# A transformer block kernel re-ordered: projections and V products between logit rounds, DMA transposes, an order computed at build

## Chip, cores, metric

The kernel runs on one core of one Trainium2 chip. The metric is the device time of one execution in microseconds (us). Every timed run quoted below was classed as fast, that is, none was more than 1.5% above the fastest of its kernel. The core's clock is the granted clock of TensorE, as a share of full speed. Engines are named as in the profile: PE is the matrix engine (PEld its weight loads, which overlap), DVE the vector engine, ACT the scalar engine, POOL GpSimd, SP the queue that issues DMAs.

## The reference, cut to what matters

```python
# x: [2048, 1024]; 32 heads of 32, 4 segments of 512 tokens, attention inside a segment
q, k, v = ln(x) @ wq, ln(x) @ wk, ln(x) @ wv
for s in range(4):
    logits = qs @ ks.T * scale + causal_mask           # 512 x 512 per head
    a_dot  = softmax(logits) @ vs
    a_mem  = (phi(qs) @ M) / (phi(qs) @ z + 1e-6)      # phi(t) = t + 1 if t > 0 else exp(t)
    o      = g * a_mem + (1 - g) * a_dot               # g = sigmoid(beta), per head
    M, z   = M + phi(ks).T @ vs, z + phi(ks).sum(tokens)
h  = x + o @ wo
z  = gelu(ln(h) @ w_in)                                # 3584 wide, halves z1 and z2
h2 = h + (z1 * (w_sp @ ln(z2) + b_sp)) @ w_out         # w_sp: 2048 x 2048 over tokens
```

Everything is bf16 with f32 accumulation. Both kernels use the same large matmuls. Counted in matmuls of 128x128 by 512 columns there are 768 for q, k and v, 256 for the output projection, 896 for w_in, 896 for w_sp and 448 for w_out: 3264 in all.

## The kernel before

Each engine's stream is written by hand. Attention works on a head group of four heads at a time (eight groups per segment). A group has four logit rounds (key blocks j = 0..3). Each round puts four heads' logits into four PSUM banks, adds the causal mask by a matmul of the identity with a triangle, and has ACT exponentiate all four banks. The next round needs the same banks, so it waits for that exponential.

```python
def L(j):                                     # one logit round of a head group
    for i in range(4):                        # four heads, side by side in the array
        P("pe", matmul(bank_f32(LB[i])[:, 0:nj], kT[32*i:32*(i+1), c, j*128:(j+1)*128],
                       qT[32*i:32*(i+1), c, 128*j:512], start=True, stop=False))
    for i in range(4):                        # the mask, added by PE
        tp = P("pe", matmul(bank_f32(LB[i])[:, 0:128], IDENT, NEGTRI, start=False, stop=True))
    ta = P("act", activation(ESALL[:, :, OFFJ[j]:...], PS[:, 0:4, 0:nj], Exp, scale=SCALE), waits=[tp])
# ...
L(0); run_extra(1)                            # extra: projections etc. of the NEXT segment
L(1); PV_emit(0); run_extra(1)                # PV_emit(cq): V product and combine of a quarter
L(2); PV_emit(1); run_extra(1)
L(3); PV_emit(2); PV_emit(3)                  # + update of M
run_extra(len(xu))

for s in range(NSEG):
    # extra units exist only where a next segment exists: segment 3 has none
    for cq_ in range(NQ):
        quad(s, cq_, per_quad[cq_])
    seg_end(s)      # 4 x (transpose 128 rows of o on PE, copy on DVE, output projection, add, store)
# w_in: two DMAs of 3.5 MB, the first released when segment 2 is done
```

All transposes (x, phi(k), o, h, w_sp) are PE transposes followed by a copy out of PSUM.

The softmax here doesn't subtract the row's maximum and nothing guards it: scores larger than these inputs give would overflow.

## Time and profile before

Median 1139.18 us of 3 runs (1135.2 to 1139.63).

From the page of the kernel before: the engine table (busy time, share of the span, instructions) and the chain of work that ended last, by engine.

```profile
PE 947.2 (83%) x6735; PEld 483.9 (42%) x6848; DVE 527.8 (46%) x1448; ACT 304.3 (27%) x383; POOL 35.2 (3%) x68
...
PE 68%; DVE 15%; ACT 6%; DMA 4%; issue 4%; POOL 1%; SPq 0%; DVEq 0%; ACTq 0%; POOLq 0%
```

The view of stretches cuts the span into the stages: start, attention up to the end of segment 2, segment 3 and its output projection, the gate layer (w_in), and the rest (w_sp and w_out). The columns are the stretch, its length, busy time of each engine with instruction counts, the granted clock, the DMA share and GB/s.

```profile
core 0: us, PE busy (x) PEld busy (x) DVE busy (x) ACT busy (x) POOL busy (x), PEclk, DMA share, GB/s
0.00:25.70 25.70, 4.16 (x33) 3.11 (x34) 13.29 (x36) 1.51 (x2) 8.12 (x21) 1.00 0.88 317
25.70:450.00 424.30, 343.99 (x3299) 182.54 (x3353) 226.71 (x750) 193.69 (x228) 8.40 (x14) 0.89 0.08 27
450.00:596.00 146.00, 87.08 (x791) 49.02 (x800) 74.11 (x268) 40.88 (x33) 1.66 (x3) 0.66 0.20 71
596.00:825.00 229.00, 209.16 (x1107) 106.89 (x1128) 99.66 (x227) 68.24 (x120) 17.05 (x30) 0.95 0.13 42
825.00:1140.20 315.20, 302.82 (x1508) 142.33 (x1536) 114.03 (x168) 0.00 (x0) 0.00 (x0) 0.99 0.16 47
```

The reader should see two things. The last two stages are nearly PE-bound at nearly full clock. The first 596 us are not: PE idles a quarter of them, and in segment 3 it also runs at two thirds of its clock.

The waits of PE name what it stood still for (total us, times, longest). Summed over the whole list, not only the five lines shown, PE waits 53.8 us for exponentials (28.0 of the 50.3 below in segment 3) and 111.4 us for DVE.

```profile
engine line waited for: us in total, times, longest us
PE ps L506 <- ACT eall L520: 50.3, 47, 2.0
PE ps L386 <- DVE oT L652: 21.6, 16, 3.1
PE ps L339 <- DVE xn_89 L352: 15.2, 4, 8.4
PE ps L339 <- DVE hn_109 L746: 13.2, 5, 7.2
PE ps L876 <- DMA wspch_115<-in_B_w_sp_dram: 10.5, 2, 6.0
```

L506 is the logits, L520 the exponential, L652 the copy of transposed o, L339 a transpose behind a layer norm. A piece of the timeline of PE in segment 3 shows what a round looks like there; in square brackets stands the idle time before the group and what ended it.

```profile
504.60 0.61 PE L506 MATMUL ps<-qT_70,kT_72 32*128 32x512 bf16 x4
505.14 0.61 PE L513 MATMUL ps<-negtri,ident 128*128 128x128 bf16 x4
507.72 0.51 PE L506 MATMUL ps<-qT_70,kT_72 32*128 32x384 bf16 x4 [1.97 <-ACT eall L520]
508.16 0.60 PE L513 MATMUL ps<-negtri,ident 128*128 128x128 bf16 x4
508.98 0.32 PE L551 MATMUL ps<-v_76,eall 128*128 128x33 bf16 x4 [0.22 <-issue]
510.31 0.40 PE L506 MATMUL ps<-qT_70,kT_72 32*128 32x256 bf16 x4 [1.00 <-ACT eall L520]
```

Waits of about 2 and 1 us stand between pieces of 1 us of work, and the work itself is slow: the clock is at 0.50.

**A ledger.** The span is split in three, from the view of stretches at 5 us steps: *idle* is the length less PE busy; *cold* is PE busy times (1 minus the granted clock), summed; *work* is the remaining PE busy. For the kernel before: idle 192.7, cold 69.4, work 877.9 us. The split is rough where records are missing (the page of e1 below shows 5261 of 5358 matmuls) and where the clock is low (e12 below shows an error of 26 us), so small differences in it prove nothing.

### The profile page before, as it was taken

How to read it: one execution, taken by the hardware profiler on the slowest of the kernel's cores; microseconds unless marked ns; L12 is line 12 of the kernel's file. 1: busy time of each engine (PE TensorE's matmuls, PEld its weight loads, DVE VectorE, ACT ScalarE, POOL GpSimd, SP SyncE). 2: the span in 40 equal slices, each digit the busy share in tenths (PEclk: the TensorE clock that was granted, in tenths of full speed). 3: DMA queues.
4: the chain of work that ended last, by engine and by line, in shares of the span. 5: the costliest groups of instructions: out<-in, count | busy, mean ns of one | idle time of the engine just before them, and what ended most of it. 6: DMA issues, size and time to landing. Idle time of an engine off the chain costs nothing.

```text
span 1140.2 us, 16027 instructions
## 1 busy us (share of the span) xinstructions
PE 947.2 (83%) x6735; PEld 483.9 (42%) x6848; DVE 527.8 (46%) x1448; ACT 304.3 (27%) x383; POOL 35.2 (3%) x68
## 2 busy tenths in 40 slices
PE   2978886688775898566749999999599999999998
PEld 1444443444333443233324545444344444444443
DVE  4066333886447853366454553632344253343332
ACT  0356651366313652144202333333100000000000
POOL 2000000000000000000000000100000000000000
PEclk9988989798985999765678999999799999999999
DMA  8010002000020004400021000000610310301102
GB/s 324 26 29 1 1 1 83 29 1 1 1 93 20 1 1 163 169 1 1 19 92 29 19 19 19 20 1 1 238 53 1 92 61 13 112 29 37 42 1 65
DMA packets 23305, 54.53 MB, mean 48 GB/s; under 512 B 2369, under 2 KB 6977, under 8 KB 23233
## 3 DMA queue, kind: packets, MB, share of 16 engines
q1 hardware_dynamic: 19152, 34.10, 9.6%
q0 software_dynamic: 4080, 19.40, 4.5%
q8 instruction: 54, 0.88, 0.3%
q14 instruction: 19, 0.15, 0.0%
HBM read 45.10 MB, written 8.39 MB: 47 GB/s over the span
## 4 chain that ended last, share of the span: by engine, by line
PE 68%; DVE 15%; ACT 6%; DMA 4%; issue 4%; POOL 1%; SPq 0%; DVEq 0%; ACTq 0%; POOLq 0%
PE ps L386 33%; PE ps L902 17%; PE ps L929 8%; ACT eall L520 4%; PE ps L513 3%; DVE stats L323 3%; PE ps L506 2%; DMA wqkv<-in_A_wv_dram 2%; PE ps L551 2%; PE ps L876 1%; DVE ta L579 1%; DVE tm L581 1%; POOL sm_58 L328 1%; PE ps L556 1%; PE ps L339 1%
## 5 line engine op out<-in xcount | busy, mean ns | idle before, releaser
L520 ACT ACTIVATE eall<-ps 128x2048 bf16<-128x2048 f32 (+3 forms) x128 | 158.6, 1239 | 173.0 <-PE ps L513 172.4
L386 PE MATMUL ps<-xnT,wqkv 128*128 128x512 bf16 x489 | 118.6, 388 | 11.3 <-DVE msum L635 4.6
L929 PE MATMUL ps<-w_out,yT 128*128 128x512 bf16 x437 | 96.8, 379 | 6.9 <-DVE yT L908 6.4
L902 PE MATMUL ps<-wspT_113,z_106 128*128 128x512 bf16 x439 | 99.1, 386 | 1.7 <-DVE wspT_113 L879 1.3
L902 PE MATMUL ps<-wspT_114,z_106 128*128 128x512 bf16 x440 | 96.6, 379 | 0.4
L905 DVE TENSOR_TENSOR tmpg<-ps,brow_120 128x512 f32<-128x512 f32 x56 | 38.7, 692 | 118.4 <-PE ps L902 103.6
L386 PE MATMUL ps<-wo,oT 128*128 128x512 bf16 x248 | 63.9, 412 | 21.8 <-DVE oT L652 21.6
L323 DVE BATCH_NORM_STATS2 stats<-z2g 128x6 f32<-128x448 bf16 x64 | 35.3, 614 | 90.9 <-ACT z2g L818 90.9
L386 PEld LDWEIGHTS ps<-xnT,wqkv 128*128 128x128 bf16 x512 | 47.3, 99 | 62.4 <-DVE msum L635 5.8
L929 PEld LDWEIGHTS ps<-w_out,yT 128*128 128x128 bf16 x448 | 43.5, 98 | 60.2 <-DVE yT L908 8.2
L902 PEld LDWEIGHTS ps<-wspT_113,z_106 128*128 128x128 bf16 x448 | 44.0, 99 | 53.9 <-issue 3.6
L902 PEld LDWEIGHTS ps<-wspT_114,z_106 128*128 128x128 bf16 x448 | 43.7, 98 | 51.9
L818 ACT ACTIVATE z2g<-ps 128x512 bf16<-128x512 f32 x64 | 34.8, 544 | 111.4 <-PE ps L386 111.4
L386 PE MATMUL ps<-wqkv,xnT 128*128 128x512 bf16 x248 | 59.0, 391 | 4.5 <-DVE msum L635 3.6
L513 PE MATMUL ps<-negtri,ident 128*128 128x128 bf16 x512 | 61.6, 256 | 0.0
L506 PE MATMUL ps<-qT_70,kT_72 32*128 32x512 bf16 (+3 forms) x256 | 25.0, 380 | 33.6 <-ACT eall L520 33.6
L386 PE MATMUL ps<-w_in_hi,hnT_103 128*128 128x512 bf16 (+1 forms) x251 | 51.6, 364 | 1.4 <-DVE hnT_103 L760 1.2
L818 ACT ACTIVATE z1T<-ps 128x512 bf16<-128x512 f32 x56 | 33.4, 597 | 70.7 <-PE ps L386 70.7
L386 PE MATMUL ps<-hnT_104,w_in_lo 128*128 128x512 bf16 x217 | 49.4, 379 | 0.4
L386 PE MATMUL ps<-w_in_hi,hnT_104 128*128 128x512 bf16 (+1 forms) x253 | 49.6, 352 | 0.2
L386 PE MATMUL ps<-hnT_103,w_in_lo 128*128 128x512 bf16 x218 | 49.3, 379 | 0.3
L386 PEld LDWEIGHTS ps<-wo,oT 128*128 128x128 bf16 x256 | 25.6, 104 | 55.2 <-issue 13.4
(138 smaller groups left out, 1073.5 us busy)
## 6 DMA issues: line engine op xcount, KB each, us to landing
wspch_115<-in_B_w_sp_dram SPq DMA_DIRECT2D x8, 512.0 KB, 4.1
wspch_122<-in_B_w_sp_dram SPq DMA_DIRECT2D x8, 512.0 KB, 4.2
hr_0_121<-out_dram SPq DMA_DIRECT2D x16, 256.0 KB, 2.8
w_in_lo<-in_B_w_in_dram POOLq DMA_DIRECT2D x1, 3584.0 KB, 12.2
w_in_hi<-in_B_w_in_dram POOLq DMA_DIRECT2D x1, 3584.0 KB, 22.8
w_out<-in_B_w_out_dram POOLq DMA_DIRECT2D x1, 3584.0 KB, 17.8
xch_87<-in_A_x_dram SPq DMA_DIRECT2D x8, 256.0 KB, 2.8
xch_88<-in_A_x_dram SPq DMA_DIRECT2D x8, 256.0 KB, 3.0
```

Source lines behind the costliest of these rows:

```text
L323: t = P("dve", (lambda e, ci=ci: e.bn_stats(STATS[:, ci, :], eng_in_ap[:, ci * csz:(ci + 1) * csz])), waits=((list(first_wait) + [chain["l ...
L328: tp = P("pool", lambda e: e.tensor_tensor(SM4[:, 1:2], SM4[:, 0:1], MHALF[:], ALU.pow), waits=[t], sig=g_pool)
L339: tok = P("pe", (lambda e, i=i: e.transpose(bb[:, i * 128:(i + 1) * 128], src_tile[:, col0 + i * 128: col0 + (i + 1) * 128], IDENT[:])), w ...
L386: tok = P("pe", (lambda e, i=i: e.matmul(dst, lhs_of_i(i), rhs_of_i(i), start=(i == 0), stop=(i == 7))), waits=(waits if i == 0 else []), ...
L506: P("pe", (lambda e, i=i, dst=dst: e.matmul(dst, kT[32 * i:32 * (i + 1), c, j * 128:(j + 1) * 128], qT[32 * i:32 * (i + 1), c, 128 * j:512 ...
L513: tp = P("pe", (lambda e, dstd=dstd: e.matmul(dstd, IDENT[:], NEGTRI[:], start=False, stop=True)), sig=(g_pe_act if i == 3 else None))
L520: ta = P("act", (lambda e: e.activation(dst4, src4, ACTF.Exp, scale=float(SCALE))), waits=wa, sig=g_act_pe)
L551: fn = (lambda e, i=i, j=j, h=h: e.matmul(dstb[:, i * 128:i * 128 + 33], ESALL[:, i, OFFJ[j] + (cq - j) * 128: OFFJ[j] + (cq - j + 1) * 12 ...
L818: t4 = P("act", (lambda e, dst=dst, o=blk["out"]: e.activation(o, dst, ACTF.Gelu_apprx_tanh)), waits=[tp] + wz, sig=g_act_dve)
L902: tok = P("pe", (lambda e, sc=sc, fc=fc, dst=dst: e.matmul(dst, Z2[:, sc, fc * 128:(fc + 1) * 128], wb[:, sc, :], start=(sc == 0), stop=(s ...
L905: t1 = P("dve", lambda e, dst=dst: e.tensor_tensor(TMPG[:], dst, BROW[0][:], ALU.add), waits=[tok, _w16(tb), tmpg_res.free], sig=g_dve_pe)
L929: tok = P("pe", (lambda e, fc=fc, half=half, tcl=tcl, dst=dst: e.matmul(dst, YT[:, fc, tcl * 128:(tcl + 1) * 128], WOUT[:, fc, half * 512: ...
```

## The change

The intent: keep PE fed throughout. The attention loop runs one head group ahead with q and k and one behind with the V product, so that each of its three logit rounds (the two shortest are merged) has independent PE work behind it. V of the next segment and the output projection of the last one are spread one group per round. The mask moves from PE to POOL, transposes go by DMA, w_in is loaded in eight blocks under segment 3, and the memory product is 132 columns wide in place of 512. PE's order is the program's; the orders of ACT, DVE, POOL and SP are computed at build by a list schedule with a cost for each operation, and the waits follow from tracked memory ranges.

```diff
+    def schedule(self):                      # at build; PE in program order, others by readiness
+        lag_same, lag_x = 30.0, 55.0
+        ... heap per engine, priority = program position ...
+            if o.dma:
+                free[e] = start + 60.0       # assumed time to issue a DMA, ns
+    def pts1(o, i, s, op):                   # assumed: 0.98 us for 1024 elements on POOL
+        G.op(POOL, ..., (150 + n_of(o)) / 1.2, name="pts1")
...
-            tp = P("pe", matmul(dstd, IDENT, NEGTRI, start=False, stop=True))
+        act(E[n % 2][...], PS[:, 0:4, 0:w], ACTF.Exp, scale=float(SCALE))
+        for j in js:                         # mask after the exponential, on POOL
+            G.op(POOL, affine_select(d, d, [[0, 4], [1, 128]], ALU.is_ge, 0.0, ...), ..., 550)
...
+    def phi(n):
+        act(ex[:, lo:hi, :], q[:, lo:hi, :], ACTF.Exp)
+        pts1(ex[:, lo:hi, :], ex[:, lo:hi, :], 1.0, ALU.min)       # POOL
+        stt(PKT[n % 2][:], q[:, 1, :], 1.0, ex[:, 1, :], ALU.add, ALU.max)
+        dma(PK[n % 3][:], PKT[n % 2][:], transpose=True)
...
+    for n in range(32):                      # n = 8 * segment + head group
+        if s >= 1 and c == 2:
+            wo_q += [(s - 1, g) for g in range(8)]                 # then one per round
+        logits(n, 0)
+        Pq(n + 1)                            # query product of the next group
+        X(n - 1)                             # V product of the last group, quarters 0 to 2
+        logits(n, 1)
+        Pk(n + 1)
+        MZU(n - 1)                           # quarter 3, memory product, update, combine
+        logits(n, 2)
+        phi(n + 1)
+        for a in vs:  v_group(*a)            # V of the next segment
+        for a in wos: wo_group(*a)           # output projection of the last segment
+        if n < 4: x_norm(4 + n)
+        if s <= 1 and c >= 4: x_norm(4 * (s + 2) + c - 4)
+        if s == 3: ... win_load(k) ...       # w_in in 8 blocks
```

(The whole kernel was rewritten in this style.)

## The prediction

> **What bounds it now.** The engine table has PE busy 947 of 1140 us (83%); the chain of waits runs over PE for 68% of the span, DVE 15%, ACT 6%, DMA 4%. Stretches: start 26 us (PE busy 4), attention to about 596 us (PE busy 431 of 570, clock 0.66 from 450 to 596), first gate layer about 596 to 809, token mixing and output layer 825 to 1140 at clock 0.96 to 1.00. Full-speed matmuls of 512 columns come every 0.216 us (49 in 10.74 us, one record in 50 missing). The last 500 us are nearly PE-bound.
>
> **Losses named by the wait list (PE).** For the exponentials 50 us, output-projection transposes through DVE 22, layer-norm chains 15+13+10+8, w_in and first weights: PE does 1.5 of 10 us from 455 to 465 while DMA moves 370 GB/s. Segment 3 has nothing between its logit rounds: 10.2 us per four heads, PE half cold (clock 0.50 from 505 to 565).
>
> **Removed from PE.** 512 mask matmuls of 128 columns (about 28 us of streaming), some 700 of 736 transposes of 128 columns (39 us), memory product 512 to 132 columns (96 times 0.16, 15 us). w_in arrives under segment 3; x, V, output projection and the last group's PV sit between logit rounds.
>
> **PE work after, at full clock (estimates from trace durations).** 3264 matmuls of 512 columns (or equivalent) x 0.2157 = 704; logits 32 x 0.95 = 30; 1280 PV matmuls x 0.045 (16 in 0.72 us) = 58; memory products and updates 12; 32 transposes 2. Sum 806.
>
> **Added around it.** Start about 9 us before the first V product plus about 4 of cold clock; last addition and store 4; waits for the last y of each block 5; gaps 5. Attention per four heads in the middle segments: PE about 10 us; ACT 0.6x3 + 1.04 + 1.88 + 1.45x2 = 7.6 us; DVE about 7.5 us; POOL about 5 us (not measured in this trace). PE should stay the bound, but only four banks rotate there, and the reciprocal-POOL-DVE chain of combine holds them: I allow 25 us of stalls. Total about 858 us.
>
> **The clock.** The Trainium skill (TensorE: Matmul & The Clock Gate, Part 1) says that an idle window drops the clock to half and that sustained work restores it. The trace agrees: 0.50 where PE sits idle over 2 us per round, 1.00 from 905 on. With dense rounds I expect 0.97 or more on average.
>
> **DMA transposes.** The skill (DMA: Bandwidth & Descriptors, latency table) gives 261 GB/s for transposes with a non-contiguous middle dimension. By estimate 0.5 us for 128 KB, 8 us per 2 MB block of w_sp plus a couple of us latency; all have 10 us or more of slack.
>
> **What would show it.** PE over 93% busy and clock over 0.96; waits for exponentials under 10 us; attention with last output projection ending near 370 us; gate layer about 193 us; mixing and output about 295 us; DMA share low.
>
> **What would make it wrong.** DMA transposes much slower, or occupying the SP queue so that loads behind them are late; POOL masking slower than about 1 us per call, or DVE and POOL blocking each other, so that combine sets the period (12 us instead of 10 would add 60 us); PE clock falling in segments 0 and 3, where rounds are thinner.
>
> Faster by over 2%: 0.98; within 2%: 0.01; slower: 0.01. Time 860 us, 8 in 10 between 830 and 920.

## The result

Median 849.34 us of 4 runs (848.38 to 850.28) against 1139.41 of 4 (1135.2 to 1140.14). The ratio is 0.7454, 95% interval 0.7431 to 0.7476. A ratio is the mean time of one kernel's fast runs over that of the other's of the same rounds, so it is not quite the ratio of the medians quoted.

The page of the changed kernel, engine table and chain by engine:

```profile
PE 800.9 (94%) x5358; PEld 384.5 (45%) x5358; DVE 368.2 (43%) x813; ACT 299.0 (35%) x343; POOL 223.2 (26%) x353
...
PE 77%; DVE 8%; POOL 7%; DMA 4%; issue 2%; ACT 2%; SPq 1%
```

Its stretches: start; attention up to the first gate product; the gate layer, which also holds the last head group's V product and the last output projection; and the rest.

```profile
core 0: us, PE busy (x) PEld busy (x) DVE busy (x) ACT busy (x) POOL busy (x), PEclk, DMA share, GB/s
0.00:15.80 15.80, 2.09 (x17) 1.76 (x18) 9.83 (x21) 1.51 (x2) 3.58 (x13) 1.00 0.89 273
15.80:345.00 329.20, 299.43 (x2914) 148.83 (x2913) 200.47 (x511) 229.25 (x221) 202.78 (x296) 0.97 0.43 106
345.00:554.00 209.00, 209.00 (x1071) 101.60 (x1070) 73.20 (x138) 67.64 (x119) 16.86 (x44) 1.00 0.25 57
554.00:847.80 293.80, 290.33 (x1359) 132.28 (x1357) 84.71 (x145) 0.60 (x1) 0.00 (x0) 1.00 0.18 46
```

From 345 us on, PE never stops until the last store. Attention shrank from some 570 us to about 330, without the last V product and output projection (some 16 us, now inside the gate layer), and its clock is 0.97.

What PE still waits for:

```profile
engine line waited for: us in total, times, longest us
PE ps L437 <- DVE xin L454: 13.7, 2, 7.9
PE ps L428 <- DMA oT<-oq: 12.2, 2, 6.8
PE ps L433 <- ACT e L440: 7.1, 6, 2.2
PE ps L428 <- DVE ta L460: 5.7, 7, 1.5
PE ps L428 <- POOL e L591: 3.5, 5, 1.4
```

The wait for the exponentials (L433 on L440) fell from 50.3 to 7.1 us. The first line is the start (the layer norm of the first x chunks). The second is new and is explained below.

The ledger of both kernels, worked out as above:

| us | before | after | difference |
|---|---|---|---|
| idle | 192.7 | 47.1 | -146 |
| cold | 69.4 | 7.0 | -62 |
| work at full clock | 877.9 | 793.9 | -84 |
| sum | 1140 | 848 | -292 |

So by this split roughly three tenths of the gain are matmuls that PE no longer does, half is idle time, and a fifth is clock that PE no longer loses. Of the idle time, waits for exponentials fell from 53.8 to 7.1 us and waits for DVE from 111.4 to 19.4. The experiments ask which part of the change removes which of these.

Two more readings of the changed kernel matter. The first is what POOL's operations cost. The groups of POOL: busy us and mean ns of one, then idle before and its releaser.

```profile
L591 POOL TENSOR_SCALAR_AFFINE_SELECT e<-e 128x512 bf16<-128x512 bf16 x128 | 93.3, 743 | 17.2 <-ACT e L440 17.2
...
L474 POOL TENSOR_SCALAR ex<-ex 128x1024 bf16<-128x1024 bf16 x16 | 44.4, 2773 | 1.5 <-ACT ex L440 0.5
```

The minimum of phi takes 2.77 us where the schedule reckons (150 + 1024) / 1.2 = 978 ns. A mask takes 0.743 us where it reckons 0.55.

The second is the longest wait for oT, in the timelines of SP and of PE:

```profile
205.06 1.19 SPq L481 DMA_TRANSPOSE pk<-pkt  x1
206.30 1.26 SPq L481 DMA_TRANSPOSE oT<-oq  x1
```

```profile
208.86 3.36 PE L428 MATMUL ps<-wo,oT 128*128 128x512 bf16 x8 [6.81 <-DMA oT<-oq]
```

This wait should not exist. The eight output-projection groups of segment 0 are popped one per round from group 2 of segment 1, so the eighth runs in round n = 17. The program text of that round puts MZU(16) ahead of it, and MZU(16) writes the o of segment 2's first heads into the same buffer (OT[s % 2]). The dependence tracker therefore makes the eighth group wait for that new o, and the trace shows it waiting: oT is issued at 206.30, PE resumes at 208.86. The kernel pays 6.8 us (and 5.4 us at the next boundary) to read a buffer that has just been overwritten; the eight matmuls after the wait then take 3.36 us, where the same eight took 1.89 a round earlier. A second slip of this kind is in the last lines of the loop: x_norm for segment s + 2 is emitted from c = 4 on and overwrites parts of the xnT buffer that the query and key products of head groups 6 and 7 of segment s, still to come, read. The trace shows this order too: the transposes of segment 2's first two chunks are issued at 75.23 and 83.17 us, the query products of head groups 6 and 7 of segment 0 follow at 78.53 and 86.25, and the first of them waited 0.25 us for that transpose. By the program, both make parts of the attention output wrong. The comparison with the reference passes all the same; no run measured the size of the error, and these are not races: every access is ordered, only in the wrong order.

### The profile page after: what moved, and what is told of

Same layout as the page of the kernel before. It is cut to its first block, busy times and chain, and to the rows that moved or that the text cites. A ratio compares the mean times of both kernels' runs of the same rounds, so it can differ in the third digit from the quotient of the medians.

```text
span 847.8 us, 12679 instructions
## 1 busy us (share of the span) xinstructions
PE 800.9 (94%) x5358; PEld 384.5 (45%) x5358; DVE 368.2 (43%) x813; ACT 299.0 (35%) x343; POOL 223.2 (26%) x353
## 2 busy tenths in 40 slices
DMA packets 128313, 64.80 MB, mean 76 GB/s; under 512 B 95488, under 2 KB 120064, under 8 KB 128256
## 4 chain that ended last, share of the span: by engine, by line
PE 77%; DVE 8%; POOL 7%; DMA 4%; issue 2%; ACT 2%; SPq 1%
PE ps L428 75%; POOL ex L474 5%; DMA xin<-in_A_x_dram 2%; PE ps L433 2%; DVE stats L512 1%; DVE pq L463 1%; DVE oq L460 1%; DVE pkt L463 1%; POOL e L591 1%; ACT e L440 1%; DVE hx L460 1%; ACT ex L440 1%; POOL rs L470 1%; DVE ta L460 1%; DMA oT<-oq 1%
## 5 line engine op out<-in xcount | busy, mean ns | idle before, releaser
L428 PE MATMUL ps<-wspT,z 128*128 128x512 bf16 x896 | 194.0, 379 | 0.0
L440 ACT ACTIVATE e<-ps 128x1536 bf16<-128x1536 f32 (+1 forms) x96 | 152.3, 1587 | 56.6 <-PE ps L433 56.5
L428 PEld LDWEIGHTS ps<-wspT,z 128*128 128x128 bf16 x896 | 87.7, 98 | 105.7
L440 ACT ACTIVATE z<-ps 128x512 bf16<-128x512 f32 x120 | 68.2, 569 | 144.7 <-PE ps L428 144.7
L591 POOL TENSOR_SCALAR_AFFINE_SELECT e<-e 128x512 bf16<-128x512 bf16 x128 | 93.3, 743 | 17.2 <-ACT e L440 17.2
L428 PE MATMUL ps<-win,hnT 128*128 128x512 bf16 (+1 forms) x512 | 97.8, 352 | 0.0
L428 PE MATMUL ps<-wout,y 128*128 128x512 bf16 (+2 forms) x462 | 97.4, 373 | 0.0
L428 PE MATMUL ps<-hnT,win 128*128 128x512 bf16 x448 | 97.3, 379 | 0.0
L428 PE MATMUL ps<-wo,oT 128*128 128x512 bf16 x256 | 63.6, 400 | 12.2 <-DMA oT<-oq 12.2
L474 POOL TENSOR_SCALAR ex<-ex 128x512 bf16<-128x512 bf16 (+1 forms) x32 | 68.5, 2142 | 18.8 <-ACT ex L440 17.1
L428 PE MATMUL ps<-xnT,wq 128*128 128x512 bf16 x256 | 62.7, 389 | 0.3 <-DMA xnT<-xin 0.3
L428 PEld LDWEIGHTS ps<-v,e 128*128 128x128 bf16 x1280 | 41.1, 96 | 13.9 <-POOL e L591 4.0
```

The source lines that it names most:

```text
L428: G.op(PE, lambda e: e.matmul(o, lhsT, rhs, start=start, stop=stop), [lhsT, rhs], [o], max(n, 60) / 2.4, lag=166, name="mm")
L440: G.op(ACT, lambda e: e.activation(o, i, func, scale=scale), [i], [o], ((172 if inps(i) else 224) + n_of(i)) / 1.2, prio=prio, name=str(func))
L474: G.op(POOL, lambda e: e.tensor_single_scalar(o, i, s, op), [i], [o], (150 + n_of(o)) / 1.2, name="pts1")
L591: G.op(POOL, lambda e, d=d: e.affine_select(d, d, [[0, 4], [1, 128]], ALU.is_ge, 0.0, base=0, channel_multiplier=-1), [d], [d], 550, name= ...
```

## The experiments

All are edits of the changed kernel, timed over 3 rounds (4 runs each), all correct by the comparison. Differences are of medians, from 849.34. The runs were on several chips; the kernel before, timed beside each, had medians from 1137.26 to 1140.12, so a difference of some 3 us says nothing.

| run | edit | median us | range | ratio to before | difference |
|---|---|---|---|---|---|
| e1 | eighth output projection one round earlier | 839.01 | 837.65 to 842.79 | 0.7372 | -10.3 |
| e2 | minimum of phi on DVE | 832.37 | 831.2 to 834.38 | 0.7311 | -17.0 |
| e3 | e1, and x norms after the last reader | 838.8 | 837.42 to 840.47 | 0.7366 | -10.5 |
| e4 | e2 and e3, x loaded first | 825.28 | 824.8 to 827.91 | 0.7253 | -24.1 |
| e5 | V and output projection clustered | 890.4 | 889.34 to 891.92 | 0.782 | +41.1 |
| e6 | V product in its own round | 864.07 | 862.12 to 865.46 | 0.7582 | +14.7 |
| e7 | mask back on PE | 872.0 | 870.51 to 872.77 | 0.7656 | +22.7 |
| e8 | x, h, w_sp transposed on PE | 896.72 | 895.05 to 901.75 | 0.7882 | +47.4 |
| e9 | w_in after attention | 856.3 | 854.5 to 859.13 | 0.7529 | +7.0 |
| e10 | e5 to e9 together | 967.39 | 966.72 to 968.12 | 0.8503 | +118.1 |
| e11 | schedule with measured costs | 836.11 | 834.83 to 839.47 | 0.7346 | -13.2 |
| e12 | e10, and projections in one burst per segment | 1101.2 | 1100.32 to 1101.84 | 0.9668 | +251.9 |

Two theories ran through them. One: PE is the bound and the change works by filling PE's waits and shedding its work, so each part undone costs its PE time or the wait that comes back. Its rival: the gain sits in one or two things (the shed work, or POOL and DMA taking over) and the order hardly matters. For the remaining waits there were two causes to tell apart: the order of the program, and POOL's slow minimum.

### e1: output projection out of the overwritten buffer's way

```diff
-            nwo = 1
+            nwo = 2 if (s in (1, 2) and c == 7) else 1
```

> One line: two output-projection groups in round 7 of segments 1 and 2, so that the eighth group no longer stands behind the V product of the next segment's first heads, which overwrites the oT buffer it reads. Theory A (the two waits of 6.8 and 5.4 us for oT come from this program order): PE's wait for oT falls from 12.2 us to under 1, time 849 to 836 to 840 us. Rival B (they come from the slow minimum on POOL, 2.8 us where the schedule reckons 1, which holds the combine back): the wait moves to another group, time within 3 us of 849. The result also becomes more exact if A is right.

Measured 839.01, and the wait for oT is gone from PE's list. Theory A holds: the two waits came from the program order. The time fell by 10.3 us, a little less than the 12.2 of the wait; in the profiled run waits for POOL's mask rose from 3.5 to 6.5 us and those for exponentials from 7.1 to 8.6. The expected gain in exactness was not measured; the comparison only says correct.

### e2: the minimum on DVE

```diff
-        pts1(ex[:, lo:hi, :], ex[:, lo:hi, :], 1.0, ALU.min)     # POOL
+        ts1(ex[:, lo:hi, :], ex[:, lo:hi, :], 1.0, ALU.min)      # DVE
```

> The minimum of phi goes from POOL to DVE, nothing else. Theory A: oT is issued about 3 us earlier, so the wait for it falls from 12.2 us to 4 to 7, and POOL busy falls from 223 to about 155 us; time 840 to 845 us. Rival B: the wait for oT disappears, and with it most of the waits for e and ta (16 us); time under 833 us.

Measured 832.37: faster than A said, about what B said, but the wait for oT did not disappear; it fell to 6.7 us, as A said. So neither was right alone. The waits for POOL's masked e (3.5 us) and for ta (5.7 us) did vanish. On DVE the minimum of 1024 elements takes 0.62 us.

There is a second effect. The operations pq and pkt read two SBUF tensors on DVE, beside POOL. In the kernel before, with POOL nearly idle, such an operation of 512 elements took 692 ns (first line); the other lines are the changed kernel's.

```profile
L406 DVE SCALAR_TENSOR_TENSOR pqT_74<-qe,pqT_74 128x512 bf16<-128x512 bf16 x16 | 11.1, 692 | 0.5
...
L463 DVE SCALAR_TENSOR_TENSOR pq<-qk,ex 128x512 bf16<-128x512 bf16 x24 | 26.5, 1103 | 6.3 <-POOL ex L474 6.3
...
L463 DVE SCALAR_TENSOR_TENSOR pkt<-qk,ex 128x512 bf16<-128x512 bf16 x24 | 22.4, 934 | 50.6 <-POOL ex L474 50.6
```

In e2 they took 902 and 738 ns. The Trainium skill (GPSIMD Engine Reference, Specifications) says that GpSimd's SBUF interfaces are shared with the vector engine, with contention for operations with two SBUF inputs; this trace agrees, and the slowdown here is 35 to 59% (934 and 1103 over 692). One by one in the timelines: the two of these 48 that met no POOL operation took 0.68 us, 44 of the 46 that met one took 0.92 to 1.13. The 50.6 us that DVE spent waiting on POOL before pkt is probably the larger item: DVE's order is fixed at build, and the second half of combine (oq) can stand behind pkt, as before the wait at 206 us, where DVE waits 1.97 us for POOL, does pkt at 204.12 and oq at 204.96.

### e3: both order slips mended

```diff
-        if n < 4:
-            x_norm(4 + n)
-        if s <= 1:
-            if c == 3: ... x_load(4 * (s + 2) + t)
-            if c >= 4: x_norm(4 * (s + 2) + c - 4)
+        if s <= 2 and c < 4:
+            x_norm(4 * (s + 1) + c)
+        if s <= 1 and c == 4: ... x_load(4 * (s + 2) + t)
```

> e1 and also the layer norm of the segment after next put after the last query and key products that read the same xnT buffer (in the changed kernel it overwrites a quarter to a half of xnT before the products of head groups 6 and 7). Same work. Theory A: as e1, 836 to 841 us; waits for xnT stay under 1 us. If the layer norms in the thinner rounds 0 to 3 of segments 1 and 2 collide with the combine, up to 8 us more. Rival (the faulty order was what made the kernel fast): over 850 us.

Measured 838.8, as e1. The right order costs nothing, so the fast time of the changed kernel does not rest on its slips.

### e4: the version that beats both

The edits of e2 and e3, and at the start:

```diff
     dma(XIN[0][:], x2d[0:128, :])
-    dma(BETAB[:], A_beta.partition_broadcast(128))
+    dma(XIN[1][:], x2d[128:256, :])
     ...
     w_half(WV, A_wv, 0)
-    x_load(1)
-    w_half(WV, A_wv, 1)
     x_load(2); x_load(3)
+    w_half(WV, A_wv, 1)
+    dma(BETAB[:], A_beta.partition_broadcast(128))
```

> e2 and e3 together, and the x chunks loaded ahead of the second half of w_v with beta last. Expected: first V product at about 9 us in place of 15.6, wait for oT gone, POOL busy about 155 us: 824 to 832 us. If start and steady rounds don't add up because the work is only pushed to the next wait: 832 to 838 us.

Measured 825.28, inside the range, though the start gave less than expected: the first V product begins at 12.67 us (15.57 in the changed kernel), not at 9. In the program the transposes of the second x chunk stand before the first V product, and DVE's order puts the statistics of the third chunk, which waits for its DMA, ahead of the second chunk's scaling.

### e5: V and output projection clustered

```diff
-            for _ in range([0, 0, 1, 1, 1, 1, 2, 2][c] if s == 0 else (0 if c == 0 else 1)):
+            for _ in range(8 if c == 7 else 0):
...
-        nwo = 0
-        if wo_q: nwo = 1 ...
+        nwo = 8 if c == 7 else 0
```

> The V and output-projection groups are all put into round 7 of each segment instead of one per round; same work, same everything else. Theory (the gain of the interleaving is idle time filled): PE busy at full clock stays at 794 us within 3, idle rises from 47 by 25 to 45 us and the clock falls somewhat in the rounds without filler, which then run at the pace of the exponentials and POOL (about 7.5 us); time 875 to 905 us. Rival (the gain is only work removed from PE): within 8 us of 849.

Measured 890.4. The ledger: idle 75.2 (up 28), cold 23.2 (up 16), work 789.6 (down 4). The top line of PE's waits answers to the 7.1 us above:

```profile
PE ps L433 <- ACT e L440: 53.1, 31, 2.2
```

The same instructions in a clustered order cost 41 us. The interleaving is worth idle time and clock, not work. The 41 us are on the low side: clustering also takes the order slip of e1 away (the wait of 12.2 us for oT is not in this list). Against e1, which is free of that slip too, the cost is 51 us.

### e6: V product not deferred

```diff
-        if n >= 1: X(n - 1)      # between rounds 0 and 1
-        if n >= 1: MZU(n - 1)    # between rounds 1 and 2
+        X(n); MZU(n)             # at the end of round n, after V and output projection
```

> The V product and combine of a head group come at the end of its own round instead of inside the next one. Same work. Theory: round 0 has only the query product (1.7 us) against an exponential of 1.9 plus logits, and in rounds without V or output projection the product waits for the last exponential and two masks, 3 us: 32 x 0.7 + 12 x 3 gives 40 to 70 us more, time 885 to 920. Rival (it doesn't matter which filler stands there): within 10 us of 849.

Measured 864.07, less than half of the cost expected. The estimate had two errors. Only 3 of the 32 rounds (n = 0, 1 and 8) have neither V nor output projection, not 12. And the query product alone nearly covers the exponential: the wait for it is 6.6 us in 22 pieces, not 0.7 us a round. What came back is the wait for the combine (14.0 us) and for the mask (12.0 us). Part of the cost is hidden, since the wait for oT fell from 12.2 to 2.3 us.

### e7: the mask on PE

```diff
+            for i in range(4):
+                mm(PS[:, i, o0:o0 + 128], IDENT[:], NEGTRI[:], False, True)
-        for j in js: G.op(POOL, affine_select(...))
```

> The causal mask goes back to PE (512 matmuls of identity and triangle, 128 columns) and off POOL. If PE is the bound: 512 x 0.056 = 29 us more work, less up to 5 us of waits for POOL: 870 to 880 us. Rival (POOL masking is what limits the rounds, so taking it away gives back what PE pays): within 10 us of 849.

Measured 872.0. Ledger: work 827.1 (up 33), idle 35.6 (down 12). POOL busy fell from 223 to 133 us. PE pays for each mask matmul, and gets a part back in waits. PE is the bound.

### e8: x, h and w_sp transposed on PE

```diff
-            dma(dst, t[:], transpose=True)
+            pend.append((dst, t))            # 8 PE transposes and a copy, one round later
...
-                dma(WSPT[...], B_w_sp[...], transpose=True)
+                dma(CH[:], B_w_sp[r:r + 128, :])    # then 16 PE transposes and 2 copies
```

> The transposes of x, h and w_sp go back to PE with DVE copies (480 more of 128 columns; those of o and phi(k) stay with DMA). If PE is the bound: 480 x 0.056 = 27 us more, plus up to 8 us where PE waits for the layer norm or for a copy: 875 to 887 us. Rival (DMA transposes cost something by contention that this gives back): below 868 us. The DMA share should fall from about 30% to under 20%.

Measured 896.72, 10 us above the range. The 27 us of work came as expected (ledger: work 820.2, up 26). The rest is waits that the DMA transposes did not have:

```profile
PE ps L428 <- DVE hnT L450: 8.6, 6, 2.5
PE ps L437 <- DMA wspch<-in_B_w_sp_dram: 7.9, 1, 7.9
...
PE ps L437 <- DVE hx L454: 5.0, 4, 2.3
```

with cold 15.0 (up 8). The profiled run was the slowest of the four, 5 us over the median, so the ledger is that much too high. PE's order is the program's, so PE stops at a transpose whose input or copy is late; in the changed kernel PE waited 0.3 us in all for the DMA transposes of x, and for those of h and w_sp not at all. The queue's DMA share fell to 21.6%, not under 20. Part of the cost is the placement that I chose for the transposes, so 47 us is an upper figure for what the DMA transposes of x, h and w_sp give.

### e9: w_in late

```diff
-            if s == 3: ... win_load(k) at c == 0 and c == 6
+    for k in range(8): win_load(k)          # after the loop, tied to the last masked exponentials
```

> The eight blocks of w_in are held back until the last masked exponentials of attention are written, as a stage boundary would; same work. Theory: the first four blocks (3.5 MB) land over about 12 us while PE needs 6 us for the first row, so PE waits 7 to 10 us and loses 1 to 3 us of clock: 857 to 862 us. Rival (loads hide behind the last V product and output projection): within 3 us of 849.

Measured 856.3, just under the range, with 4.0 us of waiting for w_in in PE's list where 7 to 10 were expected. Small, and smaller than expected.

### e10: all five undone

> e5, e6, e7, e8 and e9 together: V and output projection clustered, V product in its own round, mask on PE, x, h and w_sp transposed on PE, w_in late. The singles cost 41 + 15 + 23 + 47 and about 9 us. If they add: 849 + 135 = 984 us. If they need each other (one filler left is enough to hide most of a wait, none is not; and the clock falls when all are gone): 1000 to 1060 us. If they overlap (the same idle time counted twice): 940 to 970 us.

Measured 967.39. The singles sum to 41.1 + 14.7 + 22.7 + 47.4 + 7.0 = 132.9; together they cost 118.1. They overlap slightly, perhaps because a round that waits for exponentials has room for a mask matmul. But 1139 - 967 = 172 us of the gain were still unaccounted for, which asks for e12. The ledger of e10 (idle 81.3, cold 24.2, work 859.4) divides them (175 us between the profiled runs) into 111 of idle time, 45 of clock and 19 of work. And the wait lists show that exponentials are the small part of the idle time. In e10 PE still waits for them in two lines:

```profile
PE ps L429 <- ACT e L441: 34.7, 26, 1.7
...
PE ps L434 <- ACT e L441: 10.2, 27, 2.0
```

That is 44.9 us, against 53.8 in the kernel before. Waits for DVE are 24.2 us in e10, against 111.4 in the kernel before.

### e11: the schedule's costs

```diff
-  max(n, 60) / 2.4                     # small matmul
+  max(n, 108) / 2.4
-  (150 + n_of(o)) / 1.2                # one-input POOL operation
+  237 if n_of(o) == 1 else 250 + 2.465 * n_of(o)
-  550                                  # mask
+  743
-  free[e] = start + 60.0               # issue of a DMA
+  free[e] = start + (1230.0 if o.name == "dmaT" else 430.0)
```

> Only the numbers of the build-time schedule change, to what the trace of the changed kernel shows: POOL minimum 2.77 us for 1024 elements (it had 0.98), mask 0.743 (0.55), small matmuls 45 ns (25), 0.43 us to issue a DMA and 1.23 us a transposing one (0.06). Same instructions, PE order unchanged. If the orders built on wrong costs are what e2 repaired beyond the wait for oT: 835 to 843 us, waits of PE for POOL and DVE fall from 9 to under 4 us. If it is the POOL work itself: 846 to 852 us, the wait for oT still 10 to 13 us in both cases.

Measured 836.11, with the same instructions and the same order on PE. PE's waits:

```profile
PE ps L428 <- DMA oT<-oq: 7.3, 2, 4.9
PE ps L428 <- DVE ta L460: 2.5, 5, 0.6
...
PE ps L428 <- POOL e L591: 0.4, 1, 0.4
```

POOL busy is 229 us, no less than in the changed kernel. So 13 us, most of what e2 gained (17), can be had with POOL's work as it was, by better orders on DVE, POOL and SP. Whether it is the same gain is not shown, since e2 and e11 were not run together, and which of the five wrong costs mattered is not either. I had expected the wait for oT to stay at 10 to 13 us; it fell to 7.3; a better DVE order that issues that DMA sooner would explain it. The order slip of e1 is still in this run. The schedule's own forecast of the span was 815.6 us with the old costs and 838.9 with the new ones; the chip showed 849.34 and 836.11.

### e12: projections in a burst at the segment boundary

On top of e10 (the second exponential buffer, which e10 does not need, makes room for q and k of eight groups):

```diff
-        Pq(n + 1)                       # between rounds 0 and 1
-        Pk(n + 1)                       # between rounds 1 and 2
+        if c == 7:
+            for m in range(8): Pq(n + 1 + m); Pk(n + 1 + m)
```

> e10 with one more thing undone: the query and key products of all eight head groups of a segment come in one burst at the segment's boundary, so nothing but the head group's own V product stands between its logit rounds (as in segment 3 of the kernel before). PE work unchanged: full-clock busy stays at 859 us within 5. Theory (the part of the gain that e5 to e10 did not give back, 172 us, is idle time and cold clock between logit rounds that projections fill): the 32 rounds wait for three exponentials each, 2 to 3 us, and the clock falls: idle from 81 to 140 to 190 us, cold excess from 24 to 40 to 90, time 1050 to 1130 us. Rival (the rest lies in the segment ends, the DVE chains per quarter and the wide memory product of the kernel before): under 1010 us.

Measured 1101.2. The stretches, cut before the gate layer, show the clock (0.74):

```profile
0.00:540.00 540.00, 389.52 (x3491) 217.62 (x3512) 188.39 (x526) 227.88 (x219) 115.20 (x174) 0.74 0.18 48
540.00:1100.10 560.10, 536.47 (x2790) 262.51 (x2838) 193.55 (x349) 74.28 (x124) 19.63 (x51) 0.98 0.19 57
```

The same view of e10, in which the projections still stand between the rounds (its cut is at 400 us):

```profile
0.00:400.00 400.00, 340.69 (x3448) 183.39 (x3448) 179.96 (x520) 223.04 (x217) 111.82 (x173) 0.95 0.24 64
400.00:965.10 565.10, 542.96 (x2903) 264.68 (x2902) 195.45 (x354) 76.68 (x127) 20.46 (x53) 0.98 0.18 56
```

And PE waits for the exponentials again, for more than twice as long as in the kernel before:

```profile
PE ps L436 <- ACT e L443: 112.3, 64, 2.0
```

The last 560 us are alike in both. The first part grew by 140 us with the same matmuls (6350 weight loads in each run, of which 64 fall on the other side of the cut). The ledger: idle 173.9 (e10: 81.3), cold 92.4 (24.2), work 833.7 (859.4). The work term should not have moved and fell by 26 us, beyond the 5 us I allowed; at a clock this low the split between busy and cold is not good to better than that. The time is inside the expected range, the idle too, cold just above it. So in this loop, with the other fillers gone, the projections between the rounds are worth 134 us of idle time and clock.

This does not settle the 172 us, although e12 was made for it. The kernel before had projections of the next segment between its rounds in segments 0 to 2, and only segment 3 was bare. In e12 all four segments are bare. Its waits for exponentials are 134.3 us (the 112.3 above and 22.0 before the V product), against 53.8 in the kernel before, so e12 takes away more than the change had added; its waits for DVE are 21.3 us, against 111.4. That its time comes within 38 us of the kernel before is therefore a coincidence of two unlike sums. By the wait lists, the waits for DVE that e10 and e12 do not bring back (87 us from the kernel before to e10: copies of transposed o, layer norms ahead of transposes, combines) are the largest named part of the 172 us, as e12's rival theory had it. Not undone in any run were the DMA transposes of o and phi(k), the narrower memory product, the combines over three quarters at once, the merged last rounds, the computed orders and the segment ends spread over the rounds; how they share the 172 us stays open.

## Why the prediction was right, point by point

- **Time.** 860 predicted with 830 to 920, 849 measured. That it came so close is in part luck: work was 12 us less than the sum said and the 5 us for the last y did not appear, while the start was 6.6 us and the stalls 4.5 us more.
- **PE work removed.** Named: 28 (masks) + 39 (transposes) + 15 (memory product) = 82 us. The ledger shows 84, an agreement closer than the ledger is good for, since the kernel before lost 69 us of clock (in e12, with 92, the split was off by 26). e7 shows the mask at 33 us of work and e8 480 transposes at 26 us. The sum of 806 us of work compares with 794 in the ledger.
- **Rounds filled.** Right in kind: the exponentials' wait is 7.1 us (under 10 predicted), and e5, e6 and e12 bring it or its like back when the fillers go. The prediction named x, V, output projection and V product as fillers. Taken out singly, V and output projection cost 41 us (51 against e1) and the deferred V product 15. The projections of the next head group, which it did not name as a filler, cost 134 (e12 against e10), but with the others already gone; they were not moved alone, so the sizes can't be ranked.
- **Waits for DVE.** The prediction named 22 us for the transposes of o and 46 for layer-norm chains as losses. In the kernel before all waits for DVE sum to 111.4 us, in the changed kernel to 19.4, of which 13.7 is the start. By the wait lists this is the larger part of the idle time that went, but no run undoes it.
- **Clock.** Over 0.97 predicted, 0.987 measured. The Trainium skill (TensorE: Matmul & The Clock Gate, Part 1) says that idle windows halve the clock; the kernel before shows a halved clock in segment 3 and e12 shows it made to order: the first half of the span has 0.74. But no one long idle window is needed: in e12 the clock is 1.00 up to 60 us, falls to 0.50 by 65 and averages 0.56 from 61 to 140, where the longest gap is 2.0 us and PE is busy 60% of the time.
- **Stages.** PE over 93% busy: 94%. Mixing and output about 295 us: 293.8. Gate layer about 193: 209 with the last output projection in it (64 matmuls of 0.2157 us, 14 us), so about 195. The last output projection near 370 us: it ended at 384.7, because four rows of gate products, about 6 us each, stand before its last group. Without these 24 us, which the prediction counts in the gate layer, it would be about 361, so attention itself took some 9 us less than predicted.
- **Start.** About 9 us predicted before the first V product, 15.57 measured. The second x chunk's DMA shared the engines with half of w_v and its layer norm stood ahead of the first V product. This error of 6.6 us was mis-sized low and was covered by terms mis-sized high: no wait for the last y of a block appears (5 us allowed), and PE is full from 345 us on.
- **Stalls in attention.** 25 us allowed; the wait list has 12.2 + 7.1 + 5.7 + 3.5 + 0.7 + 0.3 = 29.5. But the reason that I gave, four rotating banks and the reciprocal chain, was only 5.7 us of it (the wait for ta). The largest item was the order slip, which I had in front of me in the diff and did not see. The number was right by luck.
- **POOL.** About 5 us per head group was too low. Minimum and four masks alone are 2.77 + 4 x 0.743 = 5.7 us, and from 130 to 303 us (segments 1 and 2) POOL is busy 63% of the time. POOL and DVE in each other's way was named as a risk; it was real, but small: taking the minimum off POOL gained 17 us (e2), and better orders with POOL's work unchanged gained 13 (e11), not the 60 that would have made the prediction wrong. How much of the 17 is blocking and how much is order is not separated.
- **DMA.** Not "low": all queues together rose from 14.4% of the engines' span (9.6, 4.5 and 0.3) to 30.5%, and 0.43 in attention. The Trainium skill (DMA: Bandwidth & Descriptors, latency table) gives 261 GB/s for transposes with a non-contiguous middle dimension; no run here measures that rate by itself. By median a transpose of 128 KB landed in 2.5 us and one of 512 KB of w_sp in 4.7, close to the estimate of 0.5 and 2 us plus a couple of us of latency. Apart from the order slip no large wait came of them, and e8 shows PE transposes, placed as they were there, to be worse.

## What to carry to other kernels

When two engines hand a buffer back and forth, put independent work of a third origin between each hand-over, and count the gain twice: the idle time and the clock that idle time takes away. Here the same matmuls in a burst instead of between the rounds cost 134 us, where no other filler was left. Then take experiments that undo the change back to the kernel before, not past it, and compare the wait lists by engine: a time that comes near the old one can be made of other waits. When an order is computed at build, check its costs against a trace and its program text for the last reader of every buffer that comes round again: five wrong costs together were worth 13 us, and a late reader cost 10 us and read the wrong data without any race.

## What the Trainium skill lacked or had wrong

- GPSIMD Engine Reference, Engine selection: it calls one-input elementwise operations on GpSimd roughly line-rate. A minimum with a constant over 128x1024 bf16, in place, took 2.77 us on POOL (2.7 ns per element) and 0.62 us on DVE (e2); ACT took 1.06 us for an exponential of the same size.
- GPSIMD Engine Reference, Specifications: it names the contention with two-input DVE operations but no size. Here a two-input operation of 512 elements went from 692 ns to 934 and 1103 ns, and to 738 and 902 ns with the minimum taken off POOL; single operations took 0.68 us with no POOL operation beside them and up to 1.13 us with one.
- DMA: Bandwidth & Descriptors gives the rate of a transposing DMA, but not for this chip how long an SBUF-to-SBUF one holds the issuing queue. In the timeline of SP a transpose of 128 KB of o took 1.26 us to issue by median (1.19 to 2.74), one of 512 KB of w_sp 2.24 us (1.76 to 3.23), against 0.33 to 0.58 us for most plain DMAs (a few took about 3).
- The same page has nothing on what many transposes cost in DMA time: in the changed kernel 95,488 of 128,313 packets were under 512 bytes (2,369 of 23,305 in the kernel before), and the share of all DMA queues went from 14.4 to 30.5% for 19% more bytes (64.8 against 54.5 MB), in a span a quarter shorter.
